# Pooled attention and a SoLU layer on one core: every load and transpose issued on SyncE, the rests of v loaded once, the weights' signs made by a Prelu slope, and a new written order

## The chip, the cores and the metric

The kernel runs on one core of a Trainium2 chip. The core has TensorE (PE, matrix products, writing to PSUM), VectorE (DVE), ScalarE (ACT), GpSimd (POOL), SyncE (SP, which here only issues DMAs), and 16 DMA engines that they share. The metric is device time in microseconds for one execution, lower is better. Before the change the median of three runs is 537.75 us (536.65 to 537.91).

## The reference, cut to what matters

The first half is attention on pooled keys and values, the second a layer with a softmax-gated activation and a layer norm:

```python
k_p = k.reshape(B, H, Sp, 8, D).mean(axis=3)      # B=8, H=8, S=576, Sp=72, D=64
v_p = v.reshape(B, H, Sp, 8, D).mean(axis=3)
scores = q @ k_p.T / 8;  attn = softmax(scores)    # over 72 pooled rows
x = (attn @ v_p) as [4608 tokens, 512]
h = x @ w_in                                       # 512 -> 1024
solu = h * softmax(h)                              # over 1024
ln = (solu - mean) / sqrt(var + 1e-6) * g_ln
out = ln @ w_out                                   # 1024 -> 512, float32
```

`w_in` and `w_out` arrive as float64 (8 bytes an element, 4.19 MB each); q, k, v and g_ln are float32.

## The kernel before

**Tiles.** The 4608 tokens are cut into 36 tiles of 128. In each group of nine tiles four belong to an even batch, one is mixed (the last 64 tokens of two batches), and four belong to the odd batch. Products keep float32 accuracy by splitting each operand into a high and a low float16 part (`q_hi`/`q_lo`, `e_hi`/`e_lo`, `x_hi`/`x_lo`, `z_hi`/`z_lo`) and adding three products: high by high, high by low, low by high. So one tile costs PE 24 matmuls of 512 columns for `mm1` (the profile's `hp`, line 785) and 24 for `mm2` (`op`, line 897), 16 small ones for the scores (`sc`, line 670) and 16 for attention times v (`xp`, line 756).

**The path of a tile.** `q_hi` (ACT), `q_lo` (DVE), a DMA transpose `qT`, scores on PE, maximum, subtraction, exponential, sum and normalisation (DVE, with the exponential on ACT), `e_hi` (ACT), `e_lo` (POOL), a DMA transpose `eT`, `xp` on PE, `x_hi` (ACT), `x_lo` (DVE), `mm1`, maximum, exponential and product (DVE, ACT, DVE), `z_cen`, `z_hi` (ACT), `z_lo` (POOL, two halves), two DMA transposes `zT`, `mm2`, evacuation (ACT), store. `hp` has two PSUM buffers, scores, `xp` and `op` one each.

**Each batch.** k and v are loaded in three pieces and pooled by POOL in halving steps (`pool_kv`, line 278). Pooled v has 576 rows; 512 of them are taken as 128 partitions by 4, and the last 16 rows of each pair of heads, the rests, make up the third piece. Before, that piece is loaded eight times, 16 partitions at a time (line 242), so that each copy lies on the partitions at which a product wants it, and is scaled by a column that selects (`sel`, `v_sel`). Powers of two that scale k, v and q come from a maximum over everything (`a_max`, `a_par`, `a_all`, `a_scale`).

**The weights.** No engine reads float64, so each weight chunk (a quarter, 1024 columns of two 32-bit words) is turned into float32 by bit operations: `w_exp` (ACT) multiplies the high word, read as float32, by 2^-111 to shift the exponent's base, `w_shift` (DVE) shifts it left by three bits, which loses the sign, `w_tail` (DVE) puts in the low word's top bits, and the sign comes back by `w_sign` (DVE, for `w_in`) or by `w_sgn` and `w_mul` (ACT, then POOL, for `w_out`). `w_bnd` sums groups of magnitudes on PE for a bound on the largest one, from which the scale follows (`w_rmax`, `w_par`, `w_all`, `wi_scale`, `wo_scale`). Then `w_hi` (ACT) writes the high part, and PE computes the low one: `w_res` multiplies the float32 weights by a scaled unit matrix (`w_dg`) and subtracts the high part, and `w_lo` (ACT) evacuates it. Two of the four chunks of `w_in` are kept in `wo`'s memory until then (`HOME`).

**The order.** Each engine runs its instructions in the written order. Before, the kernel builds a list of operations with durations, due times (`SHIFT`, `tm`) and a model of the engines, the DMA rings and the buffers, plans it in up to twelve rounds and writes the instructions in the best plan's order. The first loads (k, q, `w_in`, g) are issued by ACT, all others and all transposes by SP. A DMA signals on one of eight semaphores in turn, so that a DMA is issued only when the one eight before it has landed.

Of the kernel before, what the change touches and what calls it, by code (L numbers as in the profile page):

```python
# [19 lines left out]
DEC = 2.0**-111  # L20

SHIFT = {
    "a_all.k": -10.21,
    "a_all.q": 0.01,
    "a_all.v": -9.77,
    "a_max.k": -2.47,
    "a_max.q": -3.68,
    "a_max.v": 6.52,  # L30
    "a_par.k": 6.67,
    "a_par.q": -9.77,
    "a_par.v": -5.27,
    "a_scale.k": -49.77,
    "a_scale.q": -6.91,
    "a_scale.v": 11.11,
    "av": 0.2,
    "e_T": -31.21,
    "e_hi": 0.05,
    "e_lo": 5.3,  # L40
    "e_mul": 8.03,
    "e_rec": -1.23,
    "e_sum": -0.71,
    "g_all": -2.22,
    "g_max": -1.94,
    "g_par": -14.35,
    "h_bat": -3.12,
    "h_exp": 15.82,
    "h_max": -0.56,
    "h_mix": 6.23,  # L50
    "h_nb": 12.34,
    "k_T": 7.39,
    "k_dup": 2.93,
    "k_hi": -20.58,
    "k_lo": -0.62,
    "load_g": 0.42,
    "load_kv": 5.56,
    "load_q": -0.47,
    "load_qm": 5.25,
    "mm1": 6.24,  # L60
    "mm2": 17.69,
    "n_f": -2.36,
    "n_u": 11.76,
    "o_evac": -0.13,
    "o_store": 19.55,
    "pool_kv": 2.14,
    "q_T": 8.93,
    "q_hi": 0.35,
    "q_lo": -0.42,
    "s_exp": 15.14,  # L70
    "s_max": -1.58,
    "s_scale": -24.14,
    "s_sub": -23.81,
    "scores": -0.07,
    "v_hi": -14.36,
    "v_lo": 2.49,
    "v_put": -11.23,
    "v_sel": -0.19,
    "w_all.wi": -1.52,
    "w_all.wo": -2.71,  # L80
    "w_bnd.wi": -12.52,
    "w_bnd.wo": 11.25,
    "w_dg.wi": -12.53,
    "w_dg.wo": -11.46,
    "w_exp.wi": -0.35,
    "w_exp.wo": 3.19,
    "w_hi.wi": -0.2,
    "w_hi.wo": 0.24,
    "w_lo.wi": -24.09,
    "w_lo.wo": -2.15,  # L90
    "w_load": -0.14,
    "w_mul.wi": -23.05,
    "w_mul.wo": 8.49,
    "w_par.wi": 14.11,
    "w_par.wo": -5.21,
    "w_res.wi": -10.18,
    "w_res.wo": -1.58,
    "w_rmax.wi": -11.49,
    "w_rmax.wo": -13.22,
    "w_sgn.wi": -4.96,  # L100
    "w_sgn.wo": 0.64,
    "w_shift.wi": -1.82,
    "w_shift.wo": 1.26,
    "w_sign.wi": 0.33,
    "w_tail.wi": 0.65,
    "w_tail.wo": -13.34,
    "wi_scale": 3.13,
# [1301 lines left out]
```

## Time and profile before

| | |
|---|---|
| median of three runs | 537.75 us |
| span of the profiled execution, its own time | 540.6 us |
| PE busy | 476.6 us, 88% |
| DVE busy | 417.9 us, 77% |
| ACT busy | 326.4 us, 60% |
| POOL busy | 314.3 us, 58% |
| mean DMA traffic | 167 GB/s |

The span runs from the first to the last instruction of one profiled execution; it is 2.85 us longer than the median of the runs that were only timed. The page cuts it into 40 slices of 13.5 us; PE's busy tenths are 2029919899998899999996999999999899999996. Up to about 40 us PE has little to do, up to about 100 us it has gaps, and from then on it is nearly always busy. A stage's worth is therefore read from that stage and not from the averages.

### The profile page before, as it was taken

Reading aid. Unit: us, or ns where it says so; the run is one execution under the profiler, and the core shown is the slowest. Engines: PE = TensorE matmul, PEld = TensorE weight load, DVE = VectorE, ACT = ScalarE, POOL = GpSimd, SP = SyncE. Lnnn points to the kernel's source line nnn. Section 1 sums busy time; section 2 is a strip of 40 time slices with the busy share of each in tenths; the row PEclk is TensorE's granted clock in tenths of the full one; section 3 lists DMA queues with packets and bytes.
Section 4 is the critical chain, followed back from the end, with each engine's and each line's share of the span. In section 5 each row is a group of like instructions: output and inputs, shape, how many; then the busy total and the mean of one; then the engine's idle time right before and its main releaser. Section 6 shows DMA issues by size and latency. Waiting matters only on the chain.

```text
span 540.6 us, 9321 instructions
## 1 busy us (share of the span) xinstructions
PE 476.6 (88%) x3238; PEld 251.4 (47%) x3238; DVE 417.9 (77%) x899; ACT 326.4 (60%) x506; POOL 314.3 (58%) x441
## 2 busy tenths in 40 slices
PE   2029919899998899999996999999999899999996
PEld 1015515455554455555552555554555455555442
DVE  3578978886988578798899889899897697886430
ACT  1358269874867347765771766656776476766451
POOL 6324497876498523896496435884697344364231
PEclk9999968999999999999997999999999999999999
DMA  8875942999698975899886768994979755664433
GB/s 313 287 263 119 266 109 71 163 225 214 142 173 175 211 136 81 210 238 184 191 188 137 180 106 186 208 219 94 220 180 200 175 88 104 137 131 98 80 79 78
DMA packets 194368, 90.02 MB, mean 167 GB/s; under 512 B 169232, under 2 KB 177424, under 8 KB 193808
## 3 DMA queue, kind: packets, MB, share of 16 engines
q1 hardware_dynamic: 191024, 83.00, 72.6%
q10 hardware_dynamic: 3296, 6.43, 3.3%
q8 instruction: 25, 0.41, 0.3%
q14 instruction: 23, 0.19, 0.1%
HBM read 39.85 MB, written 9.44 MB: 91 GB/s over the span
## 4 chain that ended last, share of the span: by engine, by line
PE 61%; DMA 13%; DVE 9%; POOL 6%; issue 4%; ACT 4%; SPq 1%; ACTq 0%; POOLq 0%; DVEq 0%
PE op L897 25%; PE hp L785 24%; PE xp L756 5%; DVE q L649 4%; DMA eT<-e 4%; DMA g_sb<-in_moe_g_ln_dram 3%; DMA vr<-in_v_dram 3%; PE sc L670 3%; POOL kr L278 2%; PE res_wi L601 1%; DMA qr<-in_q_dram 1%; DMA kr<-in_k_dram 1%; DMA wor<-in_moe_w_out_dram 1%; POOL wor L478 1%; DVE z L830 1%
## 5 line engine op out<-in xcount | busy, mean ns | idle before, releaser
L785 PE MATMUL hp<-wi,xT 128*128 128x512 f16 x864 | 198.1, 382 | 4.5 <-DVE xT L768 4.4
L897 PE MATMUL op<-wo,zT 128*128 128x512 f16 x864 | 195.7, 380 | 3.9 <-DMA zT<-z 2.2
L897 PEld LDWEIGHTS <-zT 128*128 128x128 f16 x864 | 83.6, 98 | 100.3 <-issue 3.6
L785 PEld LDWEIGHTS <-xT 128*128 128x128 f16 x864 | 82.3, 98 | 96.4 <-DVE xT L768 4.9
L850 POOL TENSOR_TENSOR z<-z,z 128x512 f16<-128x512 f32 x71 | 84.4, 1207 | 52.7 <-ACT z L844 44.3
L735 POOL TENSOR_TENSOR e<-e,e 128x512 f16<-128x512 f32 x36 | 43.1, 1196 | 38.0 <-ACT e L726 37.9
L278 POOL TENSOR_TENSOR vr<-vr 128x512 f32<-128x512 f32 (+1 forms) x48 | 48.8, 1030 | 20.2 <-DMA vr<-in_v_dram 19.5
L795 DVE TENSOR_REDUCE m<-hp 128x1 f32<-128x1024 f32 x36 | 43.9, 1220 | 17.0 <-PE hp L785 16.9
L839 ACT ACTIVATE z<-z,sz 128x1024 f32<-128x1024 f32 x36 | 41.2, 1144 | 23.6 <-DVE z L830 23.5
L806 ACT ACTIVATE z<-hp,nb,Hb 128x1024 f32<-128x1024 f32 x32 | 38.4, 1199 | 26.1 <-DVE nb L798 25.7
L830 DVE SCALAR_TENSOR_TENSOR z<-hp,rs,z 128x1024 f32<-128x1024 f32 x36 | 46.1, 1281 | 8.4 <-ACT z L806 7.6
L756 PE MATMUL xp<-eT,vb 128*128 128x128 f16 (+1 forms) x640 | 39.1, 216 | 13.6 <-DMA eT<-e 12.8
L278 POOL TENSOR_TENSOR kr<-kr 128x512 f32<-128x512 f32 (+3 forms) x48 | 42.2, 895 | 15.2 <-DMA kr<-in_k_dram 14.9
L756 PEld LDWEIGHTS <-vb 128*128 128x128 f16 x640 | 35.6, 99 | 23.1 <-DMA eT<-e 15.4
L883 POOL TENSOR_TENSOR f<-V,u 128x1 f32<-128x1 f32 x36 | 7.6, 211 | 66.0 <-DVE u L875 54.1
L764 ACT ACTIVATE xT<-xp 128x512 f16<-128x512 f32 x36 | 21.4, 595 | 39.3 <-PE xp L756 39.0
L905 ACT ACTIVATE osb<-op,f 128x512 f32<-128x512 f32 x36 | 24.6, 683 | 30.2 <-PE op L897 9.8
L680 DVE TENSOR_REDUCE mx<-sc 128x8 f32<-128x576 f32 x36 | 27.1, 753 | 19.0 <-PE sc L670 18.9
L844 ACT ACTIVATE z<-z 128x1024 f16<-128x1024 f32 x36 | 37.9, 1053 | 0.7
L863 ACT ACTIVATE junk<-z 128x1024 f16<-128x1024 f32 x36 | 37.6, 1046 | 0.0
L670 PE MATMUL sc<-kT,qT 128*128 128x72 f16 (+1 forms) x640 | 27.3, 201 | 10.7 <-DMA qT<-q 8.6
L768 DVE SCALAR_TENSOR_TENSOR xT<-xp,xT 128x512 f16<-128x512 f32 x36 | 24.6, 685 | 15.1 <-ACT xT L764 15.1
(252 smaller groups left out, 672.3 us busy)
## 6 DMA issues: line engine op xcount, KB each, us to landing
vr<-in_v_dram SPq DMA_DIRECT2D x16, 512.0 KB, 5.5
out_dram<-osb SPq DMA_DIRECT2D x32, 256.0 KB, 3.2
kr<-in_k_dram SPq DMA_DIRECT2D x14, 512.0 KB, 5.4
...
wir<-in_moe_w_in_dram ACTq DMA_DIRECT2D x2, 1024.0 KB, 16.0
```

The costliest lines, as they stand in the source:

```text
L278: nc.gpsimd.tensor_tensor(out=dst, in0=src[:, :, :n], in1=src[:, :, n : 2 * n], op=ALU.add)
L670: nc.tensor.matmul(o, lhsT=t["qT"][:, h, lo:hi], rhs=kT[:, x, h * SP : (h + 1) * SP], start=(x == 0), stop=(x == 1),)
L735: nc.gpsimd.tensor_tensor(out=m[:, 1], in0=e_pair(i)[:, :, :P], in1=m[:, 0], op=ALU.subtract)
L756: nc.tensor.matmul(xp[:, c, lo:hi], lhsT=vb[b % 2][:, x, c].rearrange("p j d -> p (j d)"), rhs=eT[:, e, lo:hi], start=(n == 0), stop=(n == 3),
L785: nc.tensor.matmul(hp[:, f], lhsT=xT[:, xt, c], rhs=wi[:, wt, c, f * 512 : (f + 1) * 512], start=(c == 0 and xt == 0 and wt == 0), stop=(c ...
L795: nc.vector.tensor_reduce(out=small(i, "m"), in_=tl[i]["hp"], axis=AX.XY, op=ALU.max)
L806: nc.scalar.activation(z, t["hp"], AF.Exp, bias=t["nb"], scale=hsc(i, 0), accum_out=small(i, "se"))
L830: nc.vector.scalar_tensor_tensor(out=t["z"], in0=t["hp"], scalar=t["rs"], in1=t["z"], op0=ALU.mult, op1=ALU.mult, accum_out=small(i, "sz"),)
L839: nc.scalar.activation(t["zf"], t["zf"], AF.Identity, bias=t["sz"], scale=-float(DFF))
L844: nc.scalar.activation(t["z16"][:, 0], t["zf"], AF.Copy)
L850: eng.tensor_tensor(out=t["z16"][:, 1, fs], in0=t["zf"][:, fs], in1=t["z16"][:, 0, fs], op=ALU.subtract)
L897: nc.tensor.matmul(op_, lhsT=zT[:, zt, c], rhs=wo[:, wt, c], start=(c == 0 and zt == 0 and wt == 0), stop=(c == CO - 1 and zt == 1),)
```

## The change

- All loads go to SP's queue, the first ones too (`q="act"` is gone); ACT issues none.
- The third piece of v is loaded by two DMAs onto 32 partitions instead of eight onto 128. The copies are made later: `v_hi` and `v_lo` write a small tile `vr` at three partition offsets, `v_put` multiplies by a mask. `e_hi` writes the matching columns in two operations instead of one; `v_sel` is gone.
- `w_exp` uses Prelu with slope 2^32 on the negative side, so that the sign survives the shift. `w_sign`, `w_sgn`, `w_mul` are gone, `w_tail` writes the float32 weight itself. The largest magnitude comes from an Abs on ACT that adds up a row (`w_abs`); `w_bnd` on PE is gone.
- `w_out`'s low part is computed by DVE (`w_lo`, one operation for each half chunk); its `w_dg`, `w_res` and evacuation are gone. `w_in` keeps them.
- `q_lo` runs on POOL instead of DVE for all tiles but the first four; for that ACT scales q in place beforehand (`q_ps`). `h_bat` and `h_mix` (three columns) move from DVE to ACT.
- The raw tiles are split into two pools, and the planner is replaced by a table `ORDER` of 2255 operation numbers.

```diff
-    "a_all.k": -10.21,
...
+ORDER = (
+    1, 0, 3, 4, 2, 5, 12, 6, 7, 8, 50, 53, 10, 54, 51, 11, 52, 56, 57, 55, 58, 59, 65, 177, 9, 17,
...
-                for n in range(8):
-                    eng.dma_start(t[16 * n : 16 * n + 16, c0:c1], pairs[P:, n // 4 :: 2])
+                for n in range(2):
+                    eng.dma_start(t[16 * n : 16 * n + 16], pairs[P:, n::2])
...
-        nc.scalar.activation(u, w_word(nm, c, 1).bitcast(F32), AF.Copy, scale=DEC)
+        nc.scalar.activation(
+            u, w_word(nm, c, 1).bitcast(F32), AF.Prelu, scale=DEC, alpha=SGN
+        )
...
+        g = p1.tile([P, DFF], BF16, tag="junk", name=f"ab_{nm}{c}")
+        nc.scalar.activation(g, st["u", c], AF.Abs, accum_out=st["bnd"][:, c : c + 1])
...
     def w_lo(nm, c):
-        nc.scalar.activation(w_dst(nm, c, 1), wst[nm]["res", c], AF.Copy)
+        if (nm, c) not in LO_V:
+            nc.scalar.activation(w_dst(nm, c, 1), wst[nm]["res", c], AF.Copy)
+            return
+        for d in range(2) if nm == "wo" else (slice(0, 2),):
+            nc.vector.scalar_tensor_tensor(
+                out=w_dst(nm, c, 1)[:, d], in0=w_f32(nm, c)[:, d],
+                scalar=w_scl(nm, 2 * c + d) if nm == "wo" else w_scl(nm, 0),
+                in1=w_dst(nm, c, 0)[:, d], op0=ALU.mult, op1=ALU.subtract,
+            )
...
+        else:
+            nc.gpsimd.tensor_tensor(
+                out=q16[:, :, 1, :], in0=q_src(i), in1=q16[:, :, 0, :], op=ALU.subtract
+            )
...
-    loads_kv(0, "kr", 0.0, 0.01, "act")
+    loads_kv(0, "kr", 0.0, 0.01)
```

Three places show how the order moves. First SP at the start of the program, before: `vr` is v of batch 0, `qT` the transposed q of tiles 0, 1 and 2, `wor` the chunks of `w_out`.

```order
L239 DMA vr_173<-in_v_dram 128x2x512 x2
L242 DMA vr_173<-in_v_dram 16x2x512 x8
L657 DMA_TRANSPOSE qT_217<-q_0_188 128x8x128
L426 DMA wor_226<-in_moe_w_out_dram 128x2x1024
L426 DMA wor_228<-in_moe_w_out_dram 128x2x1024
L426 DMA wor_265<-in_moe_w_out_dram 128x2x1024
L657 DMA_TRANSPOSE qT_288<-q_1_191 128x8x128
L657 DMA_TRANSPOSE qT_351<-q_2_240 128x8x128
```

The same queue after, from its fifth row on (k and q of batch 0 stand ahead of it): `wo` and `wir` are the four chunks of `w_in`.

```order
L486 DMA wo<-in_moe_w_in_dram 128x2048
L486 DMA wir_148<-in_moe_w_in_dram 128x2048
L486 DMA wir_150<-in_moe_w_in_dram 128x2048
L298 DMA vr_1_154<-in_v_dram 128x2x512
L301 DMA vr_2_158<-in_v_dram 16x2x512 x2
L298 DMA vr_0_169<-in_v_dram 128x2x512
L713 DMA_TRANSPOSE qT_214<-q_0_201 128x8x128
L486 DMA wor_221<-in_moe_w_out_dram 128x2x1024
L486 DMA wor_224<-in_moe_w_out_dram 128x2x1024
L713 DMA_TRANSPOSE qT_229<-q_1_216 128x8x128
```

Ahead of the first transpose there were ten loads of v, eight of them small; now there are four, but also k, q and all of `w_in`.

Second POOL, before, at its 44th row: `kr` and `kp` are k of batch 1 and its pooled rows, `e` the attention of tiles 1 and 2, `wor` the chunks of `w_out` (line 478 is `w_mul`).

```order
L278 TENSOR_TENSOR kr_490<-kr_490 128x2x256
L278 TENSOR_TENSOR kr_490<-kr_490 128x2x128
L278 TENSOR_TENSOR kp_88<-kr_490 128x2x64
L278 TENSOR_TENSOR kr_490<-kr_490 128x2x256
L735 TENSOR_TENSOR e_0_95<-e_595,e_0_95 128x512
L478 TENSOR_TENSOR wor_226<-u_wo_303,sg_wo_271 128x1024
L739 TENSOR_TENSOR e_0_95<-e_595,e_0_95 128x4x16
L278 TENSOR_TENSOR kr_490<-kr_490 128x2x128
L278 TENSOR_TENSOR kr_490<-kr_490 64x256
L478 TENSOR_TENSOR wor_228<-u_wo_286,sg_wo_650 128x1024
```

POOL after, from its 48th row: the lines of `e_lo` are 794 and 798, that of `q_lo` is 706 (`q_4`, tile 4).

```order
L798 TENSOR_TENSOR e_0_98<-e_481,e_0_98 128x2x32
L335 TENSOR_TENSOR vp_93<-vr_2_361 32x128
L794 TENSOR_TENSOR e_0_98<-e_481,e_0_98 128x512
L335 TENSOR_TENSOR kr_2_476<-kr_2_476 64x256
L706 TENSOR_TENSOR q_4_566<-qm_306,q_4_566 128x8x64
L335 TENSOR_TENSOR kr_2_476<-kr_2_476 64x128
L335 TENSOR_TENSOR kr_0_493<-kr_0_493 128x2x256
L335 TENSOR_TENSOR kr_0_493<-kr_0_493 128x2x128
```

The large pieces of batch 1's k now stand behind `e_lo` of tile 2, no weight passes through POOL, and a `q_lo` stands in the row.

Third DVE, after, where `w_out`'s low parts are made (line 650, reading `wor` and the high part in `wo`): `z` is the product of tile 0's and 1's activations (line 889), `xT` is `x_lo`, `m` is `h_max`.

```order
L650 SCALAR_TENSOR_TENSOR wo<-wor_221,sg_wo,wo 128x512 x2
L877 TENSOR_SCALAR pz_719<-pz_719 128x1
L881 RECIPROCAL pz_719<-pz_719 128x1
L354 TENSOR_REDUCE amx_k<-kp_91 128x1
L883 TENSOR_SCALAR rs_754<-pz_719,Hb_590 128x1
L650 SCALAR_TENSOR_TENSOR wo<-wor_237,sg_wo,wo 128x512 x2
L889 SCALAR_TENSOR_TENSOR z_743,sz_779<-hp_579,rs_754,z_743 128x1024
L827 SCALAR_TENSOR_TENSOR xT_790<-xp_762,xT_790 128x512
L854 TENSOR_REDUCE m_798<-hp_691 128x1
```

Before, DVE has no such operation; in its place PE runs 24 matmuls of `w_res` for `w_out` between the tiles' own.

## Rows read from the trace of the kernel before

**Rows 1.** The page, busy time (share of the span) and instructions of each engine.

```profile
PE 476.6 (88%) x3238; PEld 251.4 (47%) x3238; DVE 417.9 (77%) x899; ACT 326.4 (60%) x506; POOL 314.3 (58%) x441
```

**Rows 2.** PE's timeline: start and length in us, instructions, idle time before and releaser.

```profile
28.42 1.14 PE L670 MATMUL sc<-kT,qT 128*128 128x72 f16 x16 [8.11 <-DMA qT<-q]
...
41.52 2.06 PE L601 MATMUL res_wi<-wo,dg_wi 128*128 128x512 f32 x2
...
54.12 3.63 PE L785 MATMUL hp<-wi,xT 128*128 128x512 f16 x16
...
75.34 1.89 PE L756 MATMUL xp<-eT,vb 128*128 128x128 f16 x16 [7.75 <-DMA eT<-e]
80.54 2.04 PE L601 MATMUL res_wo<-wor,dg_wo 128*128 128x512 f32 x2 [3.31 <-ACT kp L335]
...
100.55 1.89 PE L897 MATMUL op<-wo,zT 128*128 128x512 f16 x8
```

**Rows 3.** The same timeline's stalls after 170 us: first, longest and last of eight.

```profile
172.37 1.90 PE L897 MATMUL op<-wo,zT 128*128 128x512 f16 x8 [2.19 <-DMA zT<-z]
...
293.22 3.59 PE L785 MATMUL hp<-wi,xT 128*128 128x512 f16 x8 [4.42 <-DVE xT L768]
...
531.15 5.34 PE L897 MATMUL op<-wo,zT 128*128 128x512 f16 x24 [0.82 <-ACT osb L905]
```

**Rows 4.** SP's timeline at the start, columns as in rows 2.

```profile
9.66 15.42 SPq L242 DMA_DIRECT2D vr<-in_v_dram  x8
25.19 1.34 SPq L657 DMA_TRANSPOSE qT<-q  x1
```

**Rows 5.** ACT's timeline, the last chunk of `w_in` and the wait for POOL.

```profile
29.08 1.11 ACT L437 ACTIVATE u_wi<-wir 128x1024 f32<-128x1024 f32 x1
...
71.63 1.12 ACT L475 ACTIVATE sg_wo<-wor 128x1024 f16<-128x1024 f32 x1 [7.96 <-POOL wor L478]
```

**Rows 6.** POOL's timeline, the wait for batch 1's k.

```profile
61.81 2.93 POOL L278 TENSOR_TENSOR kr<-kr 128x512 f32<-128x512 f32 x2 [8.44 <-DMA kr<-in_k_dram]
```

**Rows 7.** Stretches: us, engines busy (instructions), PEclk (granted clock), DMA share, GB/s.

```profile
4.00:6.00 2.00, 0.00 (x0) 0.00 (x0) 0.00 (x0) 0.00 (x0) 1.73 (x2) 1.00 1.01 311
...
12.00:14.00 2.00, 1.60 (x6) 0.86 (x4) 0.83 (x5) 1.32 (x2) 0.00 (x0) 1.00 1.02 414
```

**Rows 8.** The same view, the stretch of the weights and the fullest one for POOL.

```profile
28.80:72.00 43.20, 30.04 (x223) 16.84 (x220) 38.90 (x71) 22.68 (x31) 17.71 (x20) 1.00 0.74 216
...
380.00:420.00 40.00, 39.37 (x274) 20.63 (x272) 33.91 (x80) 28.02 (x45) 33.24 (x46) 1.00 1.03 199
```

**Rows 9.** Groups of instructions: shapes, xcount, busy us, mean ns, idle before. DVE and ACT.

```profile
L795 DVE TENSOR_REDUCE m<-hp 128x1 f32<-128x1024 f32 x36 | 43.9, 1220 | 17.0 <-PE hp L785 16.9
L839 ACT ACTIVATE z<-z,sz 128x1024 f32<-128x1024 f32 x36 | 41.2, 1144 | 23.6 <-DVE z L830 23.5
...
L683 DVE TENSOR_TENSOR sc<-sc,mx 128x576 f32<-128x576 f32 x36 | 27.5, 765 | 1.0
...
L728 ACT ACTIVATE e<-e 128x128 f16<-128x128 f32 x36 | 10.7, 297 | 0.0
...
L813 DVE TENSOR_SCALAR pz<-nb 128x1 f32<-128x1 f32 x36 | 7.6, 211 | 0.9
...
L583 ACT ACTIVATE wo<-wor,sg_wo 128x512 f16<-128x512 f32 x8 | 5.6, 748 | 0.0
...
L690 ACT ACTIVATE sc<-sc,ct('b', 5)_3986 128x576 f32<-128x576 f32 x4 | 2.8, 710 | 4.2 <-DVE sc L683 4.2
```

**Rows 10.** The same view: `q_lo` on DVE for two batches, `z_lo` on POOL, `w_res`.

```profile
L850 POOL TENSOR_TENSOR z<-z,z 128x512 f16<-128x512 f32 x71 | 84.4, 1207 | 52.7 <-ACT z L844 44.3 <-DMA out_dram<-osb 4.8 <-DVE amx_q L297 3.5
...
L649 DVE SCALAR_TENSOR_TENSOR q<-qr,sq('b', 4)_2965,q 128x512 f16<-128x512 f32 x4 | 14.1, 3519 | 0.1
...
L601 PE MATMUL res_wo<-wor,dg_wo 128*128 128x512 f32 x16 | 10.6, 745 | 3.3 <-ACT kp L335 3.3
...
L649 DVE SCALAR_TENSOR_TENSOR q<-qr,sq('b', 0)_168,q 128x512 f16<-128x512 f32 x4 | 3.6, 900 | 0.0
```

More of the change, by code (lines that the diff above doesn't have):

```diff
@@ L20 @@
 DEC = 2.0**-111
-SHIFT = {
-    "a_all.k": -10.21,
[L26 to L107, printed above, removed]
-    "wo_scale": -12.88,
-    "x_hi": -1.88,
-    "x_lo": -13.16,
-    "z_T": -23.52,
-    "z_cen": -9.26,
-    "z_hi": 1.33,
-    "z_lo": 11.79,
-    "z_mul": 2.42,
-    "z_scale": 3.17,
-    "z_var": -6.62,
-}
+SGN = 2.0**32
+ORDER = (
[131 rows of a table added]
+)
 @with_exitstack
@@ L194 @@
     nc.gpsimd.memset(own, 1.0)
[L195 removed]
+    for n, edge in ((0, SP),):
         nc.gpsimd.affine_select(
@@ L227, with raw_key, raw_tile @@
     PIECES = {"kr": ((0, 2), (2, 4), (4, 5)), "vr": ((0, 2), (2, 4), (4, 6))}
+    def raw_key(b, which, part):
+        if b == 0:
+            return ("raw4", which, b, part)
+        return ("raw4", which, b) if part == 2 else ("raw8", which, b)
+    def raw_tile(b, which, part):
+        key = raw_key(b, which, part)
+        if key not in bat[b]:
+            n = 4 if key[0] == "raw8" else 2
+            pool = raw8 if key[0] == "raw8" else raw4
+            bat[b][key] = pool.tile([P, n, POOL * D], F32, tag=key[0], name=f"{which}{b}_{part}")
+        t = bat[b][key]
+        return t[:, 2:] if key[0] == "raw8" and part else t[:, :2]
     def load_kv(eng, b, which, part):
@@ L231, in load_kv @@
         c0, c1 = PIECES[which][part]
-        if which not in bat[b]:
-            n = NC if which == "kr" else NV
-            bat[b][which] = raw.tile([P, n, POOL * D], F32, tag="raw", name=f"{which}{b}")
-        t = bat[b][which]
+        t = raw_tile(b, which, part)
         if which == "vr":
@@ L415 @@
     HOME = (("wi", 0), ("wi", 1))
+    LO_V = tuple(("wo", c) for c in range(4))
+    DIRECT = (0, 1, 2, 3)
     U_TAG = {"wi": ("z", "z", "z16", "z16"), "wo": ("z", "z16", "z", "z16")}
@@ L520, in h_bat @@
         bat[b]["H"] = t
-        nc.vector.tensor_scalar(
-            out=t, in0=pw3, scalar1=grp["v", b]["p"], scalar2=None, op0=ALU.mult
-        )
+        nc.scalar.activation(t, pw3, AF.Copy, scale=grp["v", b]["p"])
     def h_mix(g):
@@ L529, in h_mix @@
             r_ = slice(64 * j, 64 * j + 64)
-            nc.vector.tensor_copy(out=t[r_], in_=bat[2 * g + j]["H"][r_])
+            nc.scalar.activation(t[r_], pw3[r_], AF.Copy, scale=grp["v", 2 * g + j]["p"][r_])
     def load_g(eng):
@@ L640, in q_src, with q_ps @@
         return mix[si][:, :, 0, :] if b is None else bat[b]["q"][:, :, si, :]
+    def q_ps(b, part):
+        src = mix[b][:, :, 0, :] if part is None else bat[b]["q"][:, 4 * part : 4 * part + 4]
+        key = ("m", b) if part is None else ("b", b)
+        nc.scalar.activation(src, src, AF.Copy, scale=grp["q", key]["s"])
     def q_hi(i):
@@ L1123, in loads_kv @@
             load(t + gap * part, us, load_kv, b, which, part, w=[("rp", which, b, part)],
-                 u=[("raw", which, b)], q=q, after=after)
+                 u=[raw_key(b, which, part)], q=q, after=after)
     def scale(nm, key, t, n, got):
@@ L1177, in group_q @@
         scale("q", key, t + 2.0, n, [("am", "q", key)])
+        if kind == "m":
+            op("act", 0.6, t + 3.3, q_ps, g, None, r=[("qm", g), ("sq", key)], w=[("qs", key)])
+        elif g:
+            for j in range(2):
+                op("act", 1.05, t + 3.3 + j, q_ps, g, j, r=[("qp", g, j), ("sq", key)],
+                   w=[("qs", key)], u=[("qr", g)])
         bs = [g] if kind == "b" else [2 * g, 2 * g + 1]
@@ L1370 @@
             feed_tile(i)
-    order = best_plan()
+    order = ORDER
+    done = set()
+    for n in order:
+        assert ops[n][5] <= done
+        done.add(n)
     with tc.manual_schedule():
-        for n, _, _ in order:
+        for n in order:
             ops[n][3](*ops[n][4])
```

375 lines of the change are left out of this document (122 added, 253 removed), and 130 rows, old and new, of the table ORDER.

## The prediction, made before the changed kernel was run

> **What bounds the kernel now.** I read the page first: PE is busy for 476.6 us of 540.6 [rows 1], so 64 us are the most that filling its gaps can give, and anything beyond that must come from work taken off PE. Then PE's timeline, to see where the gaps are [rows 2, 3]. There are two parts. Up to 100.55 us, when `mm2` of tile 0 begins, PE waits often: the first scores wait 8.11 us for the transposed q at 28.42, dense work begins only with `w_in`'s residuals at 41.52, `mm1` of tile 0 starts at 54.12, and then two waits of 7.75 and 3.31 us follow around 75 to 80 us, after which matmuls run at half speed for a while (2.04 us for two float32 ones at 80.54). From 100.55 on PE is full: eight stalls after 170 us add up to 13.85 us, the longest 4.42 us at 293.22, behind which eight matmuls take 3.59 instead of 1.89 us. The last matmul ends at 531.15 + 5.34 = 536.5, and 4.1 us of evacuation and store follow.
>
> So the second part is bound by PE, the first by what feeds it. Next, the timelines of the feeders. SP needs 15.42 us to issue the eight small loads of v's third piece, and the first transpose of q stands behind them at 25.19 [rows 4]. ACT can't take up the last chunk of `w_in` before 29.08, since a `q_hi` ahead of it waits for the buffer of that transpose [rows 5]. POOL waits 8.44 us for batch 1's k, with `e_lo` of tile 2 and `w_out`'s signs queued behind [rows 6]; that `e_lo` is what the 7.75 us of PE wait for, and ACT stands 7.96 us waiting for the signs [rows 5].
>
> **What the start costs after the change.** I follow the new order with durations of rows.
>
> *Loads.* Even with one queue in use the DMA engines are at their full share, 1.01 with 311 GB/s for the short rows of k and q, and 1.02 with 414 GB/s for the weights [rows 7]. So one queue loses no capacity: k and q (2.23 MB at 311 GB/s from about 2 us) land by 9, `w_in` (4.19 MB at 414) by 19, v by about 22.6, q's first transpose, behind it, by about 25. It was 28.42.
>
> *The scale of `w_in`.* DVE takes the maximum of k once POOL has pooled its last piece (about 11.3), two maxima over q at 1.22 us [rows 9], and a reduction over partitions with five small steps, 2.4 us: 16.7. Then ten large operations stand in its order up to the scale: four shifts at 0.7, four `w_tail` at 1.22, two `q_lo` at 0.76, with half a microsecond of small ones 9.7 us: 26.4. The last bound, the pass over PE and the scale take another 2.4: 28.8. ACT has nine operations of some 1.1 us in the same time and is not later. Before, the last chunk is only taken up at 29.08 [rows 5], and all of this follows it.
>
> *From there to `mm2`.* Tile 0 can enter `mm2` when two chunks of `w_out` are split. DVE's list up to that point has 8 operations of 1024 columns at 1.22 (9.8 us), 21 of 512 or 576 columns at 0.76 (16.0) and four shifts like them (3.0), four halves of the new `w_lo` at 0.75 (3.0), three maxima (1.7) and some 43 small ones at 0.21 (9.0): 42.5 us. ACT's has 21 of 1024 columns at 1.14 (23.9), four halves of `w_hi` at 0.75 (3.0), 14 at 0.71 (9.9), 14 small ones at 0.30 (4.2) and five reads of a sum at 0.2 (1.0): 42.0 us [rows 9]. POOL and PE have less. Both lists are nearly full, so the waits between them count: DVE worked 38.9 of 43.2 us in the same stretch before [rows 8], 90%. At that pace 42.5 us take 47, and `mm2` begins at 28.8 + 47 + 1 = 77 us. At 100% it would be 71, at 65% (ACT waits for DVE and the other way round, as ACT does before, with 22.7 of 43.2 us busy) 94. I take 77, near DVE's row.
>
> *What is not in the trace.* No row shows Prelu or Abs. Prelu takes the place of a Copy of 1.11 us [rows 5]; at the lower end it costs the same, at the upper end twice as much, 8 x 1.1 = 9 us on ACT, and `mm2` at 86. I take the Copy. Nor is `w_out`'s `w_lo` there; the nearest rows are `q_lo`, the same operation on the same shape, with 0.90 us for batch 0 and 3.52 for batch 4 [rows 10]. Its eight pieces cost 6 to 28 us on DVE. I take 0.75 to 0.90, since most of them stand between small operations when POOL does `z_lo` one at a time, and keep the rest for the range.
>
> **What that is worth.** Behind the start of `mm2` of tile 0 PE has the same work as before, except for the last quarter of `w_out`'s residuals (a quarter of 10.6 us [rows 10], about 2.5). Before it is 536.5 - 100.55 = 435.9 us, less 13.85 of stalls, 2.5 of residuals and 1.7 of half speed behind the stall at 293: 418 us of full work. What PE does ahead of that point, `mm1` of tiles 0 to 2, four tiles' scores and `xp`, is the same too; the other 18 of the 24 matmuls of `w_res` for `w_out` and the 64 of `w_bnd` go, from a stretch in which PE waits anyway. With the stalls and the slow matmuls of the second part left as they are: 77 + 418 + 13.9 + 1.7 + 4.1 = 514.7 us of span, 25.9 less than the 540.6 of the profiled execution. The timed runs are 2.85 us below that execution; taking the difference off their median gives 537.75 - 25.9 = 511.8, so 512.
>
> **The second part.** `q_lo` of 32 tiles leaves DVE and goes to POOL, where `z_lo`, also a subtraction of 512 columns into float16, takes 1.21 us [rows 10]: 38.6 us more for POOL. In its fullest stretch POOL is busy for 33.24 of 40 us [rows 8]; with 3.3 tiles there it comes to 37.2, so it still has 2.8 us of room, and PE stays the bound. ACT gets `q_ps` (14 x 1.14 and 4 x 0.71, 18.8 us), a second small `e_hi` for each tile (36 x 0.30, 10.8) and some 3 us for `h_bat` and `h_mix`: 33 us over 36 tiles, 0.9 a tile, against 12 us (28.0 of 40) that it has free in that stretch. I cost all this at nothing; the cover is PE's 11.8 us a tile. If it is gone, each `q_lo` costs up to its 1.21 us. The six small loads fewer for each batch also go at nothing, since SP waits more than it issues there.
>
> *A rule that bears on it.* The same `q_lo` takes 0.90 us for one batch and 3.52 for another on DVE [rows 10]. The Trainium skill, "SBUF — State Buffer", section "Who interferes with whom", says that a DVE instruction with two SBUF inputs and a GpSimd one that reads SBUF lock each other out for a whole instruction, whoever comes second waits. By that the move takes 32 such instructions from DVE, but more POOL work then locks out those that remain, `w_tail`, `v_lo` and above all the new `w_lo`, whose both inputs are in SBUF. The trace agrees with its first half; the rival below that prices `w_lo` at the slow row is what the second half would do here.
>
> **The rivals.**
>
> *The start is held up by order or queue, `mm2` at about 88 us: 523.* SP now issues everything in one row, and a transpose that waits for DVE or POOL holds up the loads of batch 1 behind it; POOL then waits for k in front of `e_lo` of tile 3 and `z_lo` as it does now. For it: the wait of 8.44 us is of that kind. Against it: v's small loads no longer stand there, and `e_lo` of tile 2 is ahead of the large pieces. Its price is that wait plus some of the 9 us of Prelu: 11 us.
>
> *`w_lo` at the slow row, `mm2` at 97: 532.* 8 x (3.52 - 0.90) = 21 us on DVE, the fuller of the two engines. For it: the slow rows are of this very shape, with POOL at work. Against it: `w_tail` and `q_lo` in the start ran mostly near their short times, and POOL waits for ACT's `z_hi` between its pieces.
>
> *The stalls of the second part go too: 500.* With DVE relieved, the stall at 293 (behind `x_lo` on DVE, 4.42 + 1.7) and the ones like it may vanish, 12 of 15.6 us. For it: the slow `q_lo` of batch 4 fall in that stretch. Against it: a new order makes new ones.
>
> *Slower, 548.* POOL becomes what PE waits for: each `q_lo` stands in front of an `e_lo` or `z_lo` of a tile whose transposes are due, and PE pays 1.1 of its 1.21 us for each of 32: 36 us, 10 more than the start gives. It decides from the point at which POOL has no room: 2.8 us in 40 are left, so it takes `q_lo` of 2.1 us instead of 1.21. For it: POOL waits as much on others as they on it. Against it: that every other POOL operation of this shape keeps to 1.2 us.
>
> **How the numbers follow.** Chances: forecast 0.57 (its own range 505 to 519, `mm2` between 71 and 84), held-up start 0.18, slow `w_lo` 0.08, stalls gone 0.11, slower 0.06. A difference under 0.3%, 1.6 us, is about what this kernel's runs can't tell from none. Faster takes the forecast, the stalls gone, and nearly all of the two smaller gains: 0.91. Same gets 0.03 from the edges of slow `w_lo`, slower 0.06. The range reaches down to 498 and up to 530: it takes in the case without stalls and the held-up start with the upper end for Prelu, and leaves out the slow case, most of slow `w_lo` and a start at 71 joined with no stalls, under 2 in 10.
>
> **What would show it.** The first scores at about 25 to 28 instead of 28.42, the scale of `w_in` near 29, `mm1` of tile 0 at 50 or a little earlier or later, `mm2` of tile 0 at 71 to 84: if it begins after 90, the start is wrong, and DVE's `w_lo` (mean over 2 us) or POOL's wait for `kr` says which. In PE's list the group `res_wo` is missing. In the second part PE's idle time between 100 us and the last matmul stays between 5 and 20 us; more than 35 us, with PE waiting for POOL's `z`, `e` or `q` through transposes, means the slower case. POOL's busy time should be near 345 us, DVE's near 370, ACT's near 360, `q_lo` on POOL near 1.2 us. The forecast is wrong if the time is above 530 or below 498.

## The result, and the profile after

The changed kernel takes 505.08 us, the median of four runs (504.27 to 507.1); the kernel before took 537.2 us beside it (four runs, 535.87 to 537.91). The ratio is 0.9416, 95% interval 0.9383 to 0.9449. The forecast was 512 us. The profiled span went from 540.6 to 501.3 us.

The page, busy time and instructions of each engine [rows 1 before]:

```profile
PE 461.1 (92%) x3150; PEld 242.8 (48%) x3150; DVE 359.2 (72%) x857; ACT 345.9 (69%) x584; POOL 334.3 (67%) x469
```

DVE lost 58.7 us, POOL and ACT gained 20.0 and 19.5, PE lost 15.5. PE's timeline (start, length, instructions, idle time before and its releaser) answers to [rows 2, 3]:

```profile
28.51 0.76 PE L363 MATMUL g_wi<-ident,g_wi 128*128 128x128 f32 x2 [9.35 <-DVE g_wi L525]
29.24 1.12 PE L726 MATMUL sc<-kT,qT 128*128 128x72 f16 x16
...
30.85 2.08 PE L638 MATMUL res_wi<-wo,dg_wi 128*128 128x512 f32 x2
...
51.18 1.90 PE L844 MATMUL hp<-wi,xT 128*128 128x512 f16 x8 [1.34 <-ACT xT L823]
...
73.41 1.67 PE L956 MATMUL op<-wo,zT 128*128 128x512 f16 x7
75.98 0.38 PE L956 MATMUL op<-wo,zT 128*128 128x512 f16 x1 [0.89 <-DVE wo L650]
77.78 0.49 PE L363 MATMUL gk<-ident,amx_k 128*128 128x128 f32 x2 [1.43 <-DVE xT L827]
...
365.20 1.90 PE L956 MATMUL op<-wo,zT 128*128 128x512 f16 x8 [0.61 <-DMA zT<-z]
...
485.80 5.34 PE L956 MATMUL op<-wo,zT 128*128 128x512 f16 x24 [0.82 <-ACT osb L964]
491.96 5.34 PE L956 MATMUL op<-wo,zT 128*128 128x512 f16 x24 [0.82 <-ACT osb L964]
```

`mm2` of tile 0 begins at 73.41 instead of 100.55. Behind it these rows hold every wait that is left, 4.57 us; before there were 14.30 (the eight stalls and one of 0.45 at 102.89). The last matmul ends at 491.96 + 5.34 = 497.30 instead of 536.49. So the 39.3 us between the spans are 27.14 of an earlier `mm2`, 9.73 of waits behind it, 2.32 of less work there, and 0.11 of the tail.

The medians are only 32.1 us apart. The timed executions took 1.7 to 3.0 us more than their spans, so the profiled execution of before took some 542 to 544 us (an estimate from its span), 5 to 6 over its median. Of that kernel's 41 timed executions five were of this longer kind, 541 to 544 us at a granted clock of 0.977 to 0.984 (the traced one's is 0.981), so its 14.30 us of waits and its begin of `mm2` are those of a long execution, and no shorter one was traced.

Stretches (us, PE, PEld, DVE, ACT, POOL busy with instructions, granted clock, DMA share, GB/s), from the scale of `w_in` to `mm2`, and the one of [rows 8]:

```profile
30.36:73.41 43.05, 37.34 (x225) 18.65 (x226) 40.16 (x89) 37.93 (x61) 27.93 (x34) 0.96 0.82 198
...
28.80:72.00 43.20, 37.49 (x225) 18.81 (x225) 39.98 (x90) 36.52 (x59) 28.00 (x35) 0.96 0.83 206
```

Between 28.8 and 72 us ACT is busy for 36.52 us, before for 22.68 [rows 8]; DVE, at 39.98, was nearly full and still is. ACT no longer waits for POOL's signs, and works beside DVE.

DVE's timeline, the way to that scale, and below it a row of POOL's, the pooling of v beside which the operation at 26.13 runs:

```profile
12.62 0.49 DVE L354 TENSOR_REDUCE amx_k<-kp 128x1 f32<-128x320 f32 x1 [10.60 <-POOL kp L335]
13.02 2.34 DVE L354 TENSOR_REDUCE amx_q<-qr 128x1 f32<-128x1024 f32 x2
...
26.13 2.17 DVE L517 SCALAR_TENSOR_TENSOR wir<-wir,u_wi 128x1024 int32<-128x1024 int32 x1
...
30.20 0.16 DVE L549 RECIPROCAL sw_wi<-pwi 128x1 f32<-128x1 f32 x1
```

```profile
24.79 6.66 POOL L335 TENSOR_TENSOR vr<-vr 128x512 f32<-128x512 f32 x4 [12.20 <-DMA vr<-in_v_dram]
```

Groups by form (count, busy us, mean ns, idle time before and its releasers), the operations that the trace of before did not hold, and `z_lo`:

```profile
L909 POOL TENSOR_TENSOR z<-z,z 128x512 f16<-128x512 f32 x71 | 82.8, 1172 | 54.9 <-ACT z L903 48.9 <-DVE sc L756 4.4 <-DVE pq('b', 3)_2315 L201 1.1
L706 POOL TENSOR_TENSOR q<-qr,q 128x512 f16<-128x512 f32 x28 | 32.3, 1157 | 9.1 <-ACT q L696 9.1
L650 DVE SCALAR_TENSOR_TENSOR wo<-wor,sg_wo,wo 128x512 f16<-128x512 f32 x8 | 8.4, 1086 | 0.0
L497 ACT ACTIVATE u_wo<-wor 128x1024 f32<-128x1024 f32 x4 | 4.4, 1137 | 0.0
L513 ACT ACTIVATE ab_wi<-u_wi 128x1024 bf16<-128x1024 f32 x4 | 4.2, 1048 | 0.1
```

Prelu (L497) takes 1.14 us, as the Copy did, Abs 1.05.

### The profile page after: what moved, and what is told of

The parts are those of the page before. It is cut to its first block, busy times and chain, and to the rows that moved or that the text cites. A ratio compares the mean times of both kernels' runs of the same rounds, so it can differ in the third digit from the quotient of the medians.

```text
span 501.3 us, 9136 instructions
## 1 busy us (share of the span) xinstructions
PE 461.1 (92%) x3150; PEld 242.8 (48%) x3150; DVE 359.2 (72%) x857; ACT 345.9 (69%) x584; POOL 334.3 (67%) x469
## 4 chain that ended last, share of the span: by engine, by line
PE 71%; DVE 12%; POOL 5%; ACT 5%; DMA 4%; issue 2%; SPq 0%; POOLq 0%; DVEq 0%; ACTq 0%
PE op L956 31%; PE hp L844 29%; PE xp L815 5%; PE sc L726 3%; DMA zT<-z 2%; POOL z L909 2%; DMA qr<-in_q_dram 1%; DVE amx_q L354 1%; DVE wor L517 1%; POOL kr L335 1%; DMA kr<-in_k_dram 1%; ACT osb L964 1%; DVE wo L650 1%; DVE m L854 1%; DVE q L701 1%
## 5 line engine op out<-in xcount | busy, mean ns | idle before, releaser
L956 PE MATMUL op<-wo,zT 128*128 128x512 f16 x864 | 198.3, 379 | 3.4 <-ACT osb L964 1.6
L956 PEld LDWEIGHTS <-zT 128*128 128x128 f16 x864 | 82.3, 98 | 95.6 <-DMA zT<-z 2.8
L909 POOL TENSOR_TENSOR z<-z,z 128x512 f16<-128x512 f32 x71 | 82.8, 1172 | 54.9 <-ACT z L903 48.9
L335 POOL TENSOR_TENSOR vr<-vr 128x512 f32<-128x512 f32 (+3 forms) x48 | 50.7, 1058 | 13.0 <-DMA vr<-in_v_dram 12.2
L750 DVE TENSOR_REDUCE sc<-sc 128x8 f32<-128x576 f32 x36 | 27.5, 763 | 19.6 <-ACT sc L746 19.5
L706 POOL TENSOR_TENSOR q<-qr,q 128x512 f16<-128x512 f32 x28 | 32.3, 1157 | 9.1 <-ACT q L696 9.1
L922 ACT ACTIVATE junk<-z 128x1024 f16<-128x1024 f32 x36 | 37.6, 1046 | 0.1
## 6 DMA issues: line engine op xcount, KB each, us to landing
wo<-in_moe_w_in_dram SPq DMA_DIRECT2D x2, 1024.0 KB, 10.6
```

The lines of the kernel that those rows point to most:

```text
L335: nc.gpsimd.tensor_tensor(out=dst, in0=src[:, :, :n], in1=src[:, :, n : 2 * n], op=ALU.add)
L909: eng.tensor_tensor(out=t["z16"][:, 1, fs], in0=t["zf"][:, fs], in1=t["z16"][:, 0, fs], op=ALU.subtract)
L922: nc.scalar.activation(junk, t["zf"], AF.Square, scale=DFF**-0.5, accum_out=small(i, "V"))
L956: nc.tensor.matmul(op_, lhsT=zT[:, zt, c], rhs=wo[:, wt, c], start=(c == 0 and zt == 0 and wt == 0), stop=(c == CO - 1 and zt == 1),)
```

## The experiments

Each ratio is to runs of the kernel before in the same session (medians 535.5 to 537.2); between sessions medians compare to some 2 us. The begin of `mm2` of tile 0 and the sum of the waits on PE's timeline behind it are from the one profiled execution of each kernel. The list of the changed kernel, with small changes at the start or none, left 4.15, 4.38 and 4.57 us of waits in three traces.

| kernel | median us | ratio to before, 95% interval | `mm2` begins | waits behind |
|---|---|---|---|---|
| before | 537.2 | 1 | 100.55 | 14.30 |
| before, planner at 0.2 us | 553.75 | 1.0342 (1.0262 to 1.0422) | 109.74 | 12.27 |
| before, planner at 0.5 us | 543.06 | 1.0134 (1.0047 to 1.0220) | 103.10 | 8.39 |
| before + `q_lo` on POOL | 539.76 | 1.0089 (1.0051 to 1.0127) | 96.47 | 12.22 |
| before + `w_lo` on DVE | 540.99 | 1.0120 (1.0074 to 1.0167) | 103.87 | 9.67 |
| before + Prelu, Abs | 519.76 | 0.9742 (0.9690 to 0.9795) | 85.31 | 3.74 |
| all edits but Prelu, old planner | 530.78 | 0.9913 (0.9883 to 0.9943) | 106.78 | 4.92 |
| all edits, old planner | 515.69 | 0.9591 (0.9530 to 0.9653) | 90.51 | 2.75 |
| all edits, old planner at 0.5 us | 519.64 | 0.9710 (0.9634 to 0.9787) | 89.02 | 5.95 |
| changed kernel | 505.08 | 0.9416 (0.9383 to 0.9449) | 73.41 | 4.57 |
| changed, `q_lo` on DVE | 512.41 | 0.9532 (0.9469 to 0.9596) | 75.12 | 7.82 |
| changed, first loads on ACT | 508.73 | 0.9466 (0.9404 to 0.9529) | 79.54 | 4.15 |
| changed, v's rests by eight loads | 514.45 | 0.9561 (0.9488 to 0.9634) | 77.58 | 11.94 |
| changed, q's maxima first | 501.40 | 0.9389 (0.9350 to 0.9428) | 70.87 | 4.38 |

**Signs by Prelu, alone.**

```diff
-        nc.scalar.activation(u, w_word(nm, c, 1).bitcast(F32), AF.Copy, scale=DEC)
+        nc.scalar.activation(
+            u, w_word(nm, c, 1).bitcast(F32), AF.Prelu, scale=DEC, alpha=SGN
+        )
...
-                bv[:, j], lhsT=up[:, j * P : (j + 1) * P], rhs=pmat4,
...
+        nc.scalar.activation(g, st["u", c], AF.Abs, accum_out=st["bnd"][:, c : c + 1])
...
-    def w_sign(nm, c):
...
-    def w_sgn(nm, c):
...
-    def w_mul(nm, c):
...
```

> The kernel before with one edit alone: the signs of the weights kept by Prelu and the bound taken by Abs with a sum on ACT, so that the signs on DVE and POOL and 64 small matmuls go; the planner makes the order. Theory A (the wait of ACT for POOL's signs, 7.96 us, and of TensorE behind it stand on the path that ends the start): mm2 of tile 0 begins 6 to 12 us earlier, time 525 to 532. Theory B (Abs costs ACT what the signs cost it, and the start is bound by loads and SP's queue): 534 to 538.

It gave 519.76 us, 15.7 less than before and below theory A's 525 to 532. PE's timeline:

```profile
52.77 1.90 PE L765 MATMUL hp<-wi,xT 128*128 128x512 f16 x8 [0.71 <-ACT xT L744]
...
85.31 1.89 PE L877 MATMUL op<-wo,zT 128*128 128x512 f16 x8
```

`mm1` of tile 0 begins 1.35 us earlier, `mm2` 15.24, more than theory A's 6 to 12: this part of the gain lies between the two, where `w_out` is made ready. PE has 3.4 us more to do behind `mm2` than before, so not all of the 15.24 is won. In the stretch of [rows 8]:

```profile
28.80:72.00 43.20, 29.16 (x138) 14.24 (x135) 36.12 (x76) 36.06 (x55) 22.66 (x27) 0.96 0.83 232
```

ACT is busy for 36.06 us there instead of 22.68; its wait of 7.96 us for POOL's signs [rows 5] is gone. The waits behind `mm2` nearly vanished too, with `q_lo` still on DVE, which was not expected of this edit. DVE's busy time fell all the same, from 417.9 to 397.0 us, 16.8 of it because the same `q_lo` of whole batches became quicker: 1.42 us in the mean for batch 4 instead of 3.52.

The edit took work from ACT, DVE, POOL and PE at once, and the planner made a new order for it. That ACT's wait is what mattered is read from these rows; it was not tried apart.

**All edits but this one.** From the kernel with all edits in the old planner's order (below) the signs were put back as they were before.

```diff
-        nc.scalar.activation(
-            u, w_word(nm, c, 1).bitcast(F32), AF.Prelu, scale=DEC, alpha=SGN
-        )
+        nc.scalar.activation(u, w_word(nm, c, 1).bitcast(F32), AF.Copy, scale=DEC)
...
+                op("pool", 2.3, t + 1.9, w_mul, nm, c, u=[rk, ("junk", nm, c)], r=[u],
+                   w=[("wf", nm, c)], after=[nt, n])
```

> All edits of the changed kernel but one, ordered by the planner of the kernel before: the weights' signs and bounds are made as in the kernel before (Copy, signs on DVE and POOL, 64 small matmuls). Theory A (Prelu and Abs carry most of what the edits bring, as the run with that edit alone says with its 16 us): 526 to 536, with mm2 of tile 0 at 98 or later. Theory B (the one queue, v's rests and w_out's low part bring the start forward by themselves, and each is enough): 516 to 522.

530.78 us, within theory A's range, 15.1 over the kernel with all edits (17 by the ratios). One row of PE's timeline:

```profile
106.78 1.89 PE L939 MATMUL op<-wo,zT 128*128 128x512 f16 x8
```

Prelu and Abs are worth 15.7 us alone and 15.1 beside the other edits. Each pair also differs in its order, and another order alone costs 7 to 18 us (below); that the two pairs agree is what speaks for the edit. The other edits together are worth about 5.

**The order.** All edits with the planner of the kernel before in place of the list (two constants of its due times, `T` and `P0`, are the changed kernel's):

```diff
-    order = ORDER
+    order = best_plan()
```

> All edits of the changed kernel, but the order is made by the planner of the kernel before (its due times and costs) in place of the list of numbers. Theory A (the edits carry the gain; order is a matter of 1 to 2%): 508 to 516, with mm2 of tile 0 beginning at 76 to 84. Theory B (the list carries more than half of the 32 us): 521 to 532. Theory C (the list carries nothing): 504 to 507.

```profile
90.51 1.67 PE L918 MATMUL op<-wo,zT 128*128 128x512 f16 x7
```

515.69 us: theory A for the time, though `mm2` begins later than it said, and fewer waits follow (2.75 us). Against it the list is worth 10.6 us by the medians and 9.4 by the ratios, all of it ahead of `mm2`. How far is that from chance? The planner has one number, the time by which a later piece of work may be preferred. It was changed in the kernel before to 0.2 and to 0.5, and to 0.5 with all edits; every instruction stays the same:

```diff
-    HOLD = 0.3
+    HOLD = 0.2
```

> The kernel before with one number of its planner changed, the time by which a later piece of work may be preferred, 0.2 for 0.3 us; every instruction is the same and only the order is another. Theory A (the stalls behind mm2 of tile 0 are an accident of the order, not of a full engine): they change by 5 us or more and the time moves by 3 us or more, either way, within 524 to 548. Theory B (they are set by DVE and POOL, whatever the order): they stay within 4 us of 15.6, time 534 to 540.

> The same with 0.5 for 0.3 us. Theory A (an accident of the order): the stalls behind mm2 of tile 0 change by 5 us or more and the time by 3 us or more, either way, within 524 to 548; the two runs need not agree. Theory B (set by the engines): the stalls stay within 4 us of 15.6, time 534 to 540.

> All edits of the changed kernel, ordered by the planner of the kernel before with 0.5 for 0.3 us as the time by which a later piece of work may be preferred. Theory A (the 10 us between the planner's order and the list of the changed kernel are beyond the spread of the planner's orders): 512 to 522. Theory B (they lie within that spread): 504 to 510 is as likely, or 524 and more the other way.

The first two gave 553.75 and 543.06, 18 and 7 us over before (the second with a wide interval, 1.0047 to 1.0220). The waits behind `mm2` went to 8.39 at 0.5, which is theory A. At 0.2 they are 12.27, within 4 us of 15.6 as theory B has it, but the time is beyond both theories; there `mm2` begins 9.2 us later, at 0.5 only 2.6. Order alone moves this kernel by up to 3%. The third gave 519.64, 4 us over its sibling, within A's range. The list's 10 us are beyond what these two orders show, but two orders are a small sample. From order to order the waits behind `mm2` stand at other places and add up to other sums. How much of that is the order and how much the single execution that was traced is not separated, and which wait is due to which row of the order was not settled; only what stands ahead of the longest stall is shown (last section).

**Two edits alone.** The first moves `q_lo` to POOL, the second `w_out`'s low part to DVE, both in the kernel before and its planner.

```diff
-        nc.vector.scalar_tensor_tensor(
-            out=q16[:, :, 1, :], in0=q_src(i), scalar=grp["q", q_key(i)]["s"],
-            in1=q16[:, :, 0, :], op0=ALU.mult, op1=ALU.subtract,
-        )
...
+            nc.gpsimd.tensor_tensor(
+                out=q16[:, :, 1, :], in0=q_src(i), in1=q16[:, :, 0, :], op=ALU.subtract
+            )
```

```diff
-        nc.scalar.activation(w_dst(nm, c, 1), wst[nm]["res", c], AF.Copy)
...
+            nc.vector.scalar_tensor_tensor(
+                out=w_dst(nm, c, 1)[:, d], in0=w_f32(nm, c)[:, d], scalar=w_scl(nm, 2 * c + d),
+                in1=w_dst(nm, c, 0)[:, d], op0=ALU.mult, op1=ALU.subtract,
+            )
```

> The kernel before with one edit alone: q of tiles 4 to 35 scaled in place by ACT and its low part taken on POOL as a plain subtract; the planner of the kernel before makes the order. Theory A (DVE's slow q_lo cause the stalls behind mm2 of tile 0): of the 15.6 us of stalls there at least 8 go, DVE's busy time falls by 40 to 55 us, time 523 to 530. Theory B (the stalls come from the order and from SP's queue, where v's small loads stand): DVE's busy time falls as much, the stalls stay above 8 us, time 533 to 541.

> The kernel before with one edit alone: the low part of w_out taken on DVE in place of TensorE's residual and ACT's copy; the planner makes the order. Theory A (the residuals of w_out, 10.6 us of TensorE and their diagonals and copies, stand on the path that ends the start): mm2 of tile 0 begins 6 to 10 us earlier than at 100.55, time 526 to 532. Theory B (they stand where TensorE waits anyway; only the last quarter, 2.5 us, comes off): 533 to 537. In both a w_lo takes 0.75 to 1.5 us on DVE.

539.76 and 540.99 us: neither is a gain. The first is theory B; the second is slower than both theories. `q_lo` on POOL took 37.6 us off DVE, 417.9 to 380.3 (the theories had 40 to 55), and the waits behind `mm2` stayed at 12.22. The stalls of before behind DVE's results, 4.42 us at 293 and 1.22 at 366, are gone; others stand in their place, most of them behind transposes, as on PE's timeline of this run:

```profile
173.70 2.83 PE L910 MATMUL op<-wo,zT 128*128 128x512 f16 x8 [2.89 <-DMA zT<-z]
...
418.70 1.07 PE L769 MATMUL xp<-eT,vb 128*128 128x128 f16 x16 [2.33 <-DMA eT<-e]
```

So in this order a lighter DVE is not enough to remove the waits. Neither loss is beyond the 7 to 18 us that another order costs, so what each edit is worth by itself stays open.

**`q_lo` back on DVE in the changed kernel.** The list is the same.

```diff
-            nc.gpsimd.tensor_tensor(
+            nc.vector.tensor_tensor(
                 out=q16[:, :, 1, :], in0=q_src(i), in1=q16[:, :, 0, :], op=ALU.subtract
```

> The changed kernel with the low part of q (tiles 4 to 35) back on DVE as a plain subtract, everything else and the list of the order as in the changed kernel. Theory A (DVE was what the second part waited for, and the 30 us of work taken off it removed 11 of the 15.6 us of stalls behind mm2 of tile 0): DVE's busy time grows by 28 to 35 us, waits of TensorE on results of DVE come back behind 100 us, and the time is 513 to 520. Theory B (the newly searched order removed them, and DVE has room at 72%): 503 to 508, no new wait over 1 us on TensorE. The begin of mm2 of tile 0 moves by less than 1.5 us in both, since tiles 0 to 3 are not touched.

512.41 us, half a microsecond under theory A's range and far from B's. DVE's busy time grew by 24.8 us, less than A's 28 to 35. Groups by form:

```profile
L706 DVE TENSOR_TENSOR q<-qr,q 128x512 f16<-128x512 f32 x28 | 26.7, 952 | 1.8 <-ACT q L696 1.8
```

The span grew by 8.1 us: `mm2` 1.71 later, not under 1.5 (DVE's list ahead of it holds one of the moved `q_lo`, 1.82 us at 59.97), 3.25 more of waits, and 3.16 more of busy PE behind `mm2`, at a granted clock of 0.98 instead of 1.00 from 75 to 150 us. Five of the waits, 1.74 us, are behind results of DVE after 100 us, where the changed kernel has none: this is theory A's mechanism, though a small part of the sum. Once the order is made for POOL, the move must stay; that is not the same as the move being a gain.

**v's rests by eight loads in the changed kernel.** The copies on partitions 32 and up are not read.

```diff
-                for n in range(2):
-                    eng.dma_start(t[16 * n : 16 * n + 16], pairs[P:, n::2])
+                for n in range(8):
+                    eng.dma_start(t[16 * n : 16 * n + 16], pairs[P:, n % 2 :: 2])
```

> The changed kernel with the rests of v loaded by eight DMAs (16 partitions each, on 128 partitions, as four copies of the same rows) in place of two on 32 partitions; nothing reads the copies, and the list of the order is the same. Theory A (SP's queue has no slack, so that six more issues ahead of each batch's transposes make TensorE wait): TensorE waits behind 100 us grow by 3 us or more, time 508 to 515. Theory B (the transfer and its issue are hidden, their removal was worth nothing): 504 to 507, with SP's queue showing 42 issues more.

514.45 us: theory A. SP's timeline of this kernel, and below it that of the changed one:

```profile
43.14 6.39 SPq L301 DMA_DIRECT2D vr<-in_v_dram  x8
49.81 1.34 SPq L805 DMA_TRANSPOSE eT<-e  x1
```

```profile
34.97 1.19 SPq L301 DMA_DIRECT2D vr<-in_v_dram  x2
...
42.41 1.36 SPq L805 DMA_TRANSPOSE eT<-e  x1
```

Eight small loads hold SP's queue for 6.39 us where two take 1.19 (some 0.42 us each to issue, and 3.0 in all of waiting for earlier DMAs to land), and the transpose of tile 0's attention stands behind them; PE then waits for it, and again later, on PE's timeline:

```profile
54.20 1.53 PE L815 MATMUL xp<-eT,vb 128*128 128x128 f16 x16 [3.47 <-DMA eT<-e]
...
280.29 1.05 PE L815 MATMUL xp<-eT,vb 128*128 128x128 f16 x16 [2.13 <-DMA eT<-e]
```

Waits for `eT` cost PE 8.1 us in all, none in the changed kernel. This includes what 3.2 MB more of transfers may cost; the two were not separated.

**The first loads on ACT's queue in the changed kernel.** k, q of batch 0, `w_in` and g; the line for k:

```diff
-    loads_kv(0, "kr", 0.0, 0.01)
+    loads_kv(0, "kr", 0.0, 0.01, q="act")
```

> The changed kernel with the first loads (k, q of batch 0, w_in, g) issued by ACT's queue as before the change, v and all transposes in SP's, same list of the order. Theory A (the queue that issues the first loads decides when the scale of w_in is ready, because the two queues share the DMA rings' rate): the scale comes 1 to 3 us later than 30.3 or earlier by as much, and the time follows by as much: 503 to 508. Theory B (the queue is indifferent: loads are bound by the rate of the 16 engines in both, and the start by the chain maxima, scale, transpose): scale within 0.7 us of 30.3, time within 1 us of 505.

508.73 us, 3.7 more, 0.7 beyond theory A's range. DVE's, ACT's and POOL's timelines:

```profile
16.42 0.49 DVE L354 TENSOR_REDUCE amx_k<-kp 128x1 f32<-128x320 f32 x1 [14.40 <-POOL kp L335]
...
27.97 2.28 DVE L517 SCALAR_TENSOR_TENSOR wir<-wir,u_wi 128x1024 int32<-128x1024 int32 x1
...
36.89 0.16 DVE L549 RECIPROCAL sw_wi<-pwi 128x1 f32<-128x1 f32 x1
```

```profile
14.41 0.83 ACTq L486 DMA_DIRECT2D wir<-in_moe_w_in_dram  x2
15.27 1.28 ACT L392 ACT_TABLE_LOAD   x1 [15.27 <-DMA kr<-in_k_dram]
```

```profile
24.21 8.82 POOL L335 TENSOR_TENSOR vr<-vr 128x512 f32<-128x512 f32 x4 [7.82 <-DMA vr<-in_v_dram]
```

The scale comes 6.7 us later, not the 1 to 3 I expected. 3.8 us of that are k's maximum, on which DVE waits at the start: v's loads on SP run beside k's. The other 2.9 come on DVE after 26 us, with no wait in between: a `q_lo`, a shift and three `w_tail` take 8.9 us there, in the changed kernel 6.0, while POOL pools v, whose first four operations take 8.82 us instead of 6.66. That ACT computes nothing until it has issued its last load at 15.2 shows too, but DVE has no wait for ACT on this way. `mm2` begins 6.1 us later. The same list was kept, though, and it was made for one queue.

**q's maxima first, in the changed kernel.** Two small edits: in the list, q's maxima ahead of k's, and what hangs on them moved up; and the output of tile 34 summed in the bank of the scores.

```diff
-    1, 0, 3, 4, 2, 5, 12, 6, 7, 8, 50, 53, 10, 54, 51, 11, 52, 56, 57, 55, 58, 59, 65, 177, 9, 17,
+    1, 0, 3, 4, 2, 5, 12, 6, 7, 8, 50, 53, 10, 54, 51, 11, 52, 177, 176, 112, 178, 179, 180, 181,
...
+            if i == NT - 2:
+                tl[i]["op"] = ps_s.tile([P, 2, 512], F32, tag="s", name=f"op{i}")[:, 0]
...
```

> The changed kernel with two small edits: in the list of the order the maxima over q stand ahead of that over k on DVE (DVE stands idle until 12.62 us for k, while q has landed), and what hangs on them moves up; and the output of tile 34 is summed in the bank of the scores, which is free by then, so that the last two tiles do not wait 0.82 us each for ACT. Theory A (DVE's order ahead of the scale of w_in sets the start, and the two waits are bare): scale 1.5 to 2.5 us earlier, two waits of 0.82 gone, time 500.5 to 503. Theory B (the loads or ACT set the scale, so that the place of the maxima is indifferent): 503 to 504.5 by the end alone.

501.40 us, in theory A's range; the ratio's interval overlaps that of the changed kernel, so of a gain over it the trace says more than the times. DVE's and PE's timelines:

```profile
10.30 2.35 DVE L354 TENSOR_REDUCE amx_q<-qr 128x1 f32<-128x1024 f32 x2 [8.29 <-DMA qr<-in_q_dram]
14.94 0.47 DVE L354 TENSOR_REDUCE amx_k<-kp 128x1 f32<-128x320 f32 x1
...
26.96 0.17 DVE L549 RECIPROCAL sw_wi<-pwi 128x1 f32<-128x1 f32 x1
```

```profile
70.87 1.67 PE L959 MATMUL op<-wo,zT 128*128 128x512 f16 x7
...
484.95 5.35 PE L959 MATMUL op<-wo,zT 128*128 128x512 f16 x24 [0.30 <-DMA zT<-z]
490.72 5.35 PE L959 MATMUL op<-wo,zT 128*128 128x512 f16 x24 [0.41 <-DMA zT<-z]
```

The scale comes 3.2 us earlier, more than the 1.5 to 2.5 expected (0.9 of it because the last `w_tail` takes 1.23 us here, ahead of POOL's work on v, and 2.17 in the changed kernel), and `mm2` 2.54; of the two waits of 0.82, waits of 0.30 and 0.41 for the transposes are left. The last matmul ends 1.23 us earlier.

## Why the prediction was right, and where it was not

- **The start.** The scale of `w_in` was put at 28.8, it came at 30.2: k's maximum stood first on DVE and waited until 12.62 for POOL, with q already landed, and one `w_tail` took 2.17 instead of 1.22 us. From there to `mm2` I gave 48 us, it took 43.05. DVE worked 40.16 of them, 93% where I took 90%, and its list was 2.3 us shorter than counted. So `mm2` began at 73.41 instead of 77, in the range of 71 to 84. The runs with and without Prelu show that this edit carried some 15 of the 32 us; that it did so through ACT's wait for the signs fits the rows, and no run took that wait away by itself. The new order carried some 10, which the prediction did not price apart. `mm1` of tile 0 came at 51.18 where I said about 50. The first scores came at 29.24 and not at 25 to 28, since PE has the reduction for the scale ahead of them.
- **The work behind it.** 418 us forecast, 419.3 measured (497.30 - 73.41 - 4.57); the tail 4.0 for 4.1.
- **The waits of the second part: the term that was mis-sized.** "With the stalls and the slow matmuls of the second part left as they are" put 13.85 + 1.7 us into the sum; 4.57 were left. This is 11 of the 13.4 us by which the forecast span of 514.7 missed 501.3. The rival with 0.11 said that they go, for the reason that DVE is relieved. They went, on top of the forecast, and the reason holds in part: the longest, at 293, stood behind one `q_lo` of 11.10 us (last section), and `q_lo` back on DVE in the changed kernel brings 3.25 us of waits. But relieving DVE alone left 12.22, since others came, and the same instructions in other orders left 8.39 to 14.30. I took waits for a property of the work which belong to one order of it, and to one execution, a long one; a change that makes the order anew throws them anew. How much each of the two gave is not shown.
- **From the span to the time.** The forecast gain of 25.9 us was taken off the median of 537.75. By the spans the gain was 39.3, by the medians 32.1, so that the long execution of before hid half of the miss. That the forecast of 512 came as near as 7 us is luck to that extent.
- **Costs at nothing.** Prelu took 1.14 us for the Copy's 1.11 [rows 5], as chosen. `q_lo` on POOL took 1.16 us for 1.2, PE had no wait for it, and the slower rival did not happen. `w_lo` took 1.09 us in the mean (0.74 in the median, 1.77 at most), above the 0.75 to 0.90 taken. The slow row was misread: 3.52 us is the mean of four `q_lo`, one of 11.10 us and three of 0.74 to 1.44, and no price for each of eight. DVE ended at 359.2 for 370, ACT at 345.9 for 360, POOL at 334.3 for 345.
- **"The six small loads fewer for each batch also go at nothing"** was wrong in the new order: putting them back costs 9.4 us by the medians, 7.8 by the ratios. I looked at SP's mean load, where it waits more than it issues, and not at what stands behind the eight issues, although [rows 4] showed that very picture at the start (most of its 15.42 us are waits for earlier loads to land; one issue takes 0.31 to 0.42).
- **One queue.** That it loses no capacity held: in the stretches of 2 us from 14 to 20 us it moves 406 to 418 GB/s, before both queues moved 407 to 421 there. The 414 GB/s of [rows 7] that I took for one queue is such a row, with loads of v from SP beside ACT's.
